# One token of gated attention and a Mish layer: the result as 256 columns in four rows, stored in 16 rows of 1 KB

## The chip, the cores and the metric

The kernel runs on one core of a Trainium2 chip. The metric is the device time of one execution in microseconds (us). The core has five engines that run side by side and wait for each other by semaphores: TensorE (PE; its weight loads are shown as PEld), VectorE (DVE), ScalarE (ACT), GpSimd (POOL) and SyncE (SP), which here only issues transfers. A transfer is split over 16 DMA engines. SBUF is the working memory of 128 partitions; TensorE writes its sums to PSUM, from where VectorE or ScalarE has to copy them before they can be stored.

## What is computed

Two branches start from the same `x` (2 batches, 512 features, float32) and are mixed by a gate:

```python
g = _sigmoid((x * gate_w).sum(-1, keepdims=True))
a = _A_ref(x, A_k_cache, A_v_cache, A_wq, A_wo)
b = _B_ref(x, B_w1, B_b1, B_w2)
return g * a + (1 - g) * b
```

`_A_ref` is attention with one query per batch: `q = x @ wq` gives 32 heads of 128, which share 8 key-value heads in fours; scores against the last 4096 positions of the key cache, softmax, the weighted sum of the values, and the product with `wo` (4096 x 512). `_B_ref` is `mish(x @ w1 + b1) @ w2` with 1792 hidden features, so `w2` is 1792 x 512. The result is 2 x 512. Some 91 MB of float32 weights and caches have to be read for it.

## The kernel before

**Loads.** SyncE issues nearly every load, in order, into three SBUF buffers of 64 KB per partition that are used in turn (`stream`): the query weights, eight pairs of keys and values, then `w12` (most of `w1`, the first part of `wo`, the first seven 128-row blocks of `w2`) and the rest of `wo`. The last loads are four pieces of `in_w2` (lines 337 to 341): rows 7 to 10 (a row here is one of the 14 blocks of 128 hidden features, 512 columns wide), rows 11 and 12, and row 13 in two halves of 128 KB each. `flat` (line 311) yields for each piece its columns and its place in the flat input. A piece with several rows has one contiguous run in memory per partition.

**Groups of columns.** All matmuls of this kernel that matter have a stationary operand of 32 columns, so that four of them go to four column groups of TensorE: group j writes partitions 32j to 32j+31 of the PSUM tile. Only two of the 32 columns hold the two batches; the others are zero (`padded`, line 108 on).

**The end.** `project` (line 349) adds up in `acc` the attention output times `wo` and the first seven rows of `w2`: here the four groups split the sum's terms, not its columns, and so `acc` holds four partial sums of 512 columns. ScalarE copies it to `asum` (line 377). A matmul with `fold2` then adds the four up. From there the groups split the result's columns: group j has columns 128j to 128j+127.

- `finish(lhsT, rhs)` (line 358) adds one row into `fin`, 128 partitions x 128 columns, with four matmuls. It is called for rows 7 to 10, for `asum`, and for row 11.
- VectorE copies `fin` to `base` (line 400).
- `half(f, h, x0, step)` (line 386) adds rows 12 and 13 into two other sums, `own_pt` and `own_q`, of 64 columns per group each. Row 13's first half is loaded ahead of its second, so that `own_pt` can be done before the last piece has come.
- `result(h)` (line 393) adds `base` and one of the two sums into `res`, on VectorE.
- The stationary operand has its two columns at the end of the 32 for even groups and at the start for odd ones (`y = j % 2 * (Q - B)`). The result thus lies in partitions 30 and 31, 32 and 33, 94 and 95, 96 and 97.
- The store (line 412) writes `res[24:104]`, 80 rows of 512 bytes; the host picks the eight rows that count. It is issued by SyncE, with a semaphore of its own, on which GpSimd waits at the very end (line 484). The `landed` instruction (line 407) lets SyncE see the last nine loads land ahead of the store.

The order of the matmuls is the order of the program where they are wrapped in `pin`. The pool `work` (line 65) has the tag `p` with two buffers, used in turn by `qs` (two), `p` (eight), `hs`, `asum` and `base`.

Of the kernel before, what the change touches and what calls it, by code (L numbers as in the profile page):

```python
# [8 lines left out]
F32 = mybir.dt.float32  # L9
AF = mybir.ActivationFunctionType  # L10
ALU = mybir.AluOpType
AX = mybir.AxisListType

P = 128
B = 2
D = 512
# [8 lines left out]
NJ = 4  # L25
NT = 4
Q = 32
# [4 lines left out]
FC = F // P  # L32
# [14 lines left out]
SCALE = DH ** -0.5  # L47
CAP = 20.0
CUTS = (0, 7, 11, 13, 14)
PART = P // 2  # L50
WO = (1, 6, 8)
ROWS = (24, 104)
WIDE = 2 * Q - B
AHEAD = W1 + WO[0] * REP * D

# [2 lines left out]
def decode_kernel(ctx: ExitStack, tc: tile.TileContext, res, stored, small, wqh, wqt, kv_in, w12, wo, w2, *rest):  # L58
    *parts, before, behind, out = rest
    nc = tc.nc  # L60
# [1 line left out]
    stream = ctx.enter_context(tc.tile_pool(name="stream", bufs=3))  # L62
    const = ctx.enter_context(tc.tile_pool(name="const", bufs=1))
    single = ctx.enter_context(tc.tile_pool(name="single", bufs=1))
    work = ctx.enter_context(tc.tile_pool(name="work", bufs=2))
    ps_s = ctx.enter_context(tc.tile_pool(name="ps_s", bufs=2, space=bass.MemoryType.PSUM))
    ps_1 = ctx.enter_context(tc.tile_pool(name="ps_1", bufs=1, space=bass.MemoryType.PSUM))

# [2 lines left out]
    def load(name, *parts):  # L71
        t = stream.tile([P, 2 * CHUNK], F32, tag="s", name=name)
        x = 0
        for cols, src in parts:
            loads.append(nc.sync.dma_start(t[:, x : x + cols], src))  # L75
            x += cols
        return t
# [36 lines left out]
    oT, actT, act2, fold2 = (padded[:, sum(sizes[:k]) : sum(sizes[: k + 1])] for k in range(len(sizes)))  # L114
    oT = oT.rearrange("p (k q) -> p k q", q=Q)
    actT = actT.rearrange("p (f q) -> p f q", q=Q)
    act2 = act2.rearrange("p (f q) -> p f q", q=WIDE)
# [41 lines left out]
    pin = tc.keep_in_program_order  # L159

    def scores(kv, t):
        sc = ps_s.tile([P, 512], F32, tag="sc", name=f"sc{kv}")
        for m in range(BN):
            for j in range(NJ):
                nc.tensor.matmul(sc[Q * j : Q * j + Q, :], qz[:, kv, m * Q : m * Q + Q],  # L165
                                 t[:, (m * NJ + j) * 512 : (m * NJ + j + 1) * 512],
                                 start=(m == 0), stop=(m == BN - 1))
        nc.vector.tensor_reduce(mx[:, kv : kv + 1], sc, axis=AX.X, op=ALU.max, negate=True)  # L168
        p = work.tile([P, 512], F32, tag="p", name=f"p{kv}")
        nc.scalar.activation(p, sc, AF.Exp, bias=mx[:, kv : kv + 1], accum_out=ls[:, kv : kv + 1])  # L170
        return p
# [125 lines left out]
    for kv in range(HKV):  # L297
        t = load(f"kv{kv}", (2 * CHUNK, kv_in[kv][:, : 2 * CHUNK]))
        p = scores(kv, t[:, :CHUNK])
# [9 lines left out]
    w12_t = load("w12", (AHEAD + CUTS[1] * D, w12))  # L309

    def flat(src, cuts, size):
        for f0, f1 in zip(cuts, cuts[1:]):
            yield (f1 - f0) * size, src[f0 * size * P : f1 * size * P].rearrange("(p x) -> p x", p=P)

    wo_t = stream.tile([P, 2 * CHUNK], F32, tag="s", name="wo")
    x = (WO[-1] - WO[0]) * REP * D
# [16 lines left out]
    x = 0  # L333
# [1 line left out]
        loads.append(nc.sync.dma_start(wo_t[:, x : x + cols], src))  # L335
        x += cols
    x = AHEAD + CUTS[1] * D
    pieces = [2 * (f - CUTS[1]) for f in CUTS[1:]]
    for cols, src in flat(w2, [*pieces[:-1], pieces[-1] - 1, pieces[-1]], D // 2):
        loads.append(nc.sync.dma_start(w12_t[:, x : x + cols], src))  # L340
        x += cols
    hidden(w12_t)
    outputs(kf, r)

    acc = ps_1.tile([P, D], F32, tag="acc", name="acc")
    fin = ps_1.tile([P, P], F32, tag="fin", name="fin")
    n_col = [0] * NJ

    def project(j, lhsT, rhs, n):
# [2 lines left out]
                                start=(n_col[j] == 1), stop=(n_col[j] == n))  # L352

    n_of = [HKV + len(range(j, CUTS[1], NJ)) for j in range(NJ)]
    n_fin = FC - CUTS[1] - 1
    done = [0]

    def finish(lhsT, rhs):
        for j in range(NJ):
            y = j % 2 * (Q - B)  # L360
            nc.tensor.matmul(fin[Q * j : Q * j + Q, :], lhsT[:, y : y + Q], rhs[:, j * P : (j + 1) * P],  # L361
                             start=(done[0] == 0), stop=(done[0] == n_fin - 1))
        done[0] += 1

    def middle(f0, f1):
        for f in range(f0, f1):
            x = AHEAD + f * D
            pin(project(f % NJ, actT[:, f, :], w12_t[:, x : x + D], n_of[f % NJ]))

    first = WO[0] * REP  # L370
# [5 lines left out]
    asum = work.tile([P, D], F32, tag="p", name="asum")  # L376
    nc.scalar.copy(asum, acc)

    def output(f0, f1):
        for f in range(f0, f1):  # L380
            x = AHEAD + f * D
            finish(act2[:, f - CUTS[1], :], w12_t[:, x : x + D])

    own = [ps_1.tile([P, PART], F32, tag=tag, name=f"own_{tag}") for tag in ("pt", "q")]

    def half(f, h, x0, step):
        for j in range(NJ):
            x, y = x0 + j * step, j % 2 * (Q - B)
            pin(nc.tensor.matmul(own[h][Q * j : Q * j + Q, :], act2[:, f - CUTS[1], y : y + Q],
                                 w12_t[:, x : x + PART], start=(f == FC - 2), stop=(f == FC - 1)))  # L390

    def result(h):
        cols = slice(h * PART, (h + 1) * PART)
        return pin(nc.vector.tensor_tensor(res[:, cols], base[:, cols], own[h], op=ALU.add))

    output(CUTS[1], CUTS[2])
    finish(fold2, asum)
    output(CUTS[2], FC - 2)
    base = work.tile([P, D], F32, tag="p", name="base")[:, :P]
    pin(nc.vector.tensor_copy(base, fin))  # L400
    for h in range(2):
        half(FC - 2, h, AHEAD + (FC - 2) * D + h * PART, P)
    for h in range(2):
        half(FC - 1, h, AHEAD + (FC - 1) * D + h * D // 2, PART)
        copy = result(h)

    landed = nc.sync.nop()
    for ld in loads[-9:]:
        tc.add_manual_dep(landed.ins, ld.ins.name,
                          mybir.DependencyInfo(mybir.DependencyClass.Sync, mybir.DependencyReason.DATA),  # L410
                          reason="SyncE sees the last loads land ahead of the store")
    store = nc.sync.dma_start(out, res[ROWS[0] : ROWS[1]]).then_inc(stored, 16)
    tc.no_tile_sem_insts.add(store.ins.name)
# [76 lines left out]
```

## Time and profile before

| | us |
|---|---|
| time, median of 3 runs (lowest to highest) | 218.78 (218.69 to 218.85) |
| the profiled execution | 218.85 |
| its span, first to last instruction | 217.0 |
| PE busy | 117.1 (54%) |
| DVE busy | 22.0 (10%) |
| ACT busy | 15.5 (7%) |
| POOL busy | 11.4 (5%) |
| moved by DMA | 91.38 MB, mean 421 GB/s |

Times in the profile are from the start of the span. A busy engine is not necessarily one that matters: the chain of waits tells which work ended last, and idle time of an engine off that chain costs nothing. In a row of the timeline stand the start, the time from there to the end of the group, the engine, the line of the program, the operation, what it writes and reads, the shape, and in brackets the idle time before it and what ended it. A group merges like instructions that follow each other, and groups can overlap. In a row of the windows stand, behind the window's length, the busy time of PE, PEld, DVE, ACT and POOL with their counts, the granted TensorE clock as a share of full speed, the share of the DMA engines that was busy, and GB/s.

### The profile page before, as it was taken

The page shows a single profiled execution, that of the slowest core. Times are in us where ns is not written, and L with a number is a line of the kernel's source. Part 1 is how long each engine was busy: PE and PEld are TensorE (multiplying, and loading weights), DVE is VectorE, ACT ScalarE, POOL GpSimd, SP SyncE. Part 2 cuts the span into 40 slices and gives each one's busy share as a digit, 9 for nine tenths or more (in the row PEclk, how much of TensorE's full clock was granted, in tenths as well). Part 3 has the DMA queues.
Part 4 walks back from the last instruction along what each step waited for, and adds up shares of the span by engine and source line. Part 5 has one row for each costly group of instructions (what it writes and reads, how often), then busy time and mean ns, then how long its engine had stood idle before and what let it go on. Part 6 is the DMA issues. An engine that isn't in the chain of part 4 may idle for free.

```text
span 217.0 us, 1884 instructions
## 1 busy us (share of the span) xinstructions
PE 117.1 (54%) x836; PEld 34.2 (16%) x836; DVE 22.0 (10%) x35; ACT 15.5 (7%) x34; POOL 11.4 (5%) x34
## 2 busy tenths in 40 slices
PE   0000786277046609543863754186166819769995
PEld 0000221012011102100120110012011201224333
DVE  0000000010001230100105010010501000260101
ACT  0200011011001000200020020002001000301001
POOL 8000100000000000000000000000000050101200
PEclk9999999589959985995669699669757697999699
DMA  9798988899989998999999899989998999999894
GB/s 362 338 507 351 571 387 387 387 559 399 399 387 544 411 399 387 532 414 399 399 519 414 387 423 459 471 387 423 450 471 387 435 447 437 422 385 468 381 404 162
DMA packets 2896, 91.38 MB, mean 421 GB/s; under 512 B 582, under 2 KB 918, under 8 KB 1098
## 3 DMA queue, kind: packets, MB, share of 16 engines
q1 hardware_dynamic: 2746, 91.24, 97.7%
q8 instruction: 6, 0.10, 0.2%
q0 software_dynamic: 144, 0.05, 0.1%
HBM read 91.24 MB, written 0.04 MB: 421 GB/s over the span
## 4 chain that ended last, share of the span: by engine, by line
DMA 76%; PE 17%; ACT 2%; SPq 2%; DVE 1%; issue 1%; POOL 1%; DVEq 0%; ACTq 0%
DMA kv<-in_kv 60%; DMA w<-in_w 16%; PE sc L165 8%; PE o L189 6%; ACT p L170 1%; DVE mx L168 1%; SPq L322 1%; PE pp L177 1%; ACT pT L178 1%; PE fin L361 1%; POOL wo L318 1%; SPq L335 0%; SPq L75 0%; SPq L81 0%; DVE base L400 0%
## 5 line engine op out<-in xcount | busy, mean ns | idle before, releaser
L165 PE MATMUL sc<-kv,qz 128*32 128x512 f32 x256 | 46.0, 884 | 51.5 <-DMA kv<-in_kv 51.5
L189 PE MATMUL o<-kv,pT 128*32 128x512 f32 x256 | 32.5, 647 | 5.8 <-ACT pT L178 5.8
L165 PEld LDWEIGHTS sc<-kv,qz 128*32 128x32 f32 x256 | 10.2, 155 | 86.2 <-DMA kv<-in_kv 58.1
L145 PE MATMUL qp<-wq,x 128*32 128x512 f32 x64 | 10.7, 712 | 23.0 <-POOL x L108 23.0
L168 DVE TENSOR_REDUCE mx<-sc 128x1 f32<-128x512 f32 x8 | 5.5, 691 | 113.2 <-PE sc L165 113.2
L170 ACT ACTIVATE p<-sc,mx 128x512 f32<-128x512 f32 x8 | 5.5, 687 | 133.5 <-DVE mx L168 133.5
L177 PE MATMUL pp<-ident,p 128*128 128x128 f32 x32 | 5.2, 286 | 12.1 <-ACT p L170 12.1
L189 PEld LDWEIGHTS o<-kv,pT 128*32 128x32 f32 x256 | 7.7, 117 | 23.5 <-issue 15.7
L318 POOL MEMSET wo<- 128x1536 f32 x1 | 1.4, 1377 | 147.6 <-PE o L189 147.6
L199 DVE TENSOR_REDUCE od<-om 128x256 f32<-128x1024 f32 x4 | 7.6, 1906 | 0.1
L196 DVE TENSOR_TENSOR om<-o,pick 128x1024 f32<-128x1024 f32 x4 | 4.9, 1225 | 20.7 <-PE o L189 20.7
L351 PE MATMUL acc<-wo,padded 128*32 128x512 f32 x56 | 6.8, 597 | 0.0
L145 PEld LDWEIGHTS qp<-wq,x 128*32 128x32 f32 x64 | 2.3, 127 | 28.1 <-POOL x L108 23.0
L177 PEld LDWEIGHTS pp<-ident,p 128*128 128x128 f32 x32 | 3.3, 140 | 19.0 <-ACT p L170 19.0
L178 ACT COPY pT<-pp 128x512 f32<-128x512 f32 x8 | 4.7, 585 | 6.2 <-PE pp L177 6.2
L351 PE MATMUL acc<-w,padded 128*32 128x512 f32 x22 | 4.5, 904 | 0.4 <-DVE padded L243 0.4
L260 PE MATMUL hp<-w,x 128*32 128x512 f32 (+1 forms) x30 | 3.6, 540 | 1.8 <-DMA w<-in_w 1.8
L351 PEld LDWEIGHTS acc<-wo,padded 128*32 128x32 f32 x56 | 2.3, 112 | 4.4 <-issue 2.8
L260 PE MATMUL hp<-wo,x 128*32 128x512 f32 x6 | 2.7, 592 | 0.0
L151 PE MATMUL qt<-ident,qs 128*128 128x128 f32 x8 | 1.3, 286 | 1.4 <-ACT qs L148 1.4
L127 DVE TENSOR_REDUCE xs<-xg 128x2 f32<-128x8 f32 x1 | 0.2, 161 | 18.2 <-POOL xg L125 18.2
L241 PE MATMUL ol<-kf,od 128*128 128x8 f32 x16 | 1.9, 253 | 0.0
(78 smaller groups left out, 35.0 us busy)
## 6 DMA issues: line engine op xcount, KB each, us to landing
wq<-in_wqt SPq DMA_DIRECT2D x1, 7168.0 KB, 21.3
w<-in_w SPq DMA_DIRECT2D x1, 6144.0 KB, 40.6
wo<-in_wo SPq DMA_DIRECT2D x1, 5120.0 KB, 27.9
wo<-in_wo SPq DMA_DIRECT2D x1, 2048.0 KB, 32.3
wq<-in_wqh SPq DMA_DIRECT2D x1, 1024.0 KB, 4.9
w<-in_w SPq DMA_DIRECT2D x1, 1024.0 KB, 34.3
w<-in_w SPq DMA_DIRECT2D x1, 512.0 KB, 35.0
w<-in_w SPq DMA_DIRECT2D x2, 128.0 KB, 21.2
```

The lines of the kernel that those rows point to most:

```text
L145: nc.tensor.matmul(qp[Q * k : Q * k + Q, :], x32[:, c, :], w[:, c, k, :], start=(c == 0), stop=(c == DC - 1))
L165: nc.tensor.matmul(sc[Q * j : Q * j + Q, :], qz[:, kv, m * Q : m * Q + Q], t[:, (m * NJ + j) * 512 : (m * NJ + j + 1) * 512], start=(m == ...
L168: nc.vector.tensor_reduce(mx[:, kv : kv + 1], sc, axis=AX.X, op=ALU.max, negate=True)
L170: nc.scalar.activation(p, sc, AF.Exp, bias=mx[:, kv : kv + 1], accum_out=ls[:, kv : kv + 1])
L177: pin(nc.tensor.transpose(pp[:, c, :], p[:, c * P : (c + 1) * P], ident))
L178: nc.scalar.copy(pT, pp)
L189: pin(nc.tensor.matmul(o[Q * j : Q * j + Q], pT[:, c, Q * j : Q * j + Q], t[:, (c * NJ + j) * 512 : (c * NJ + j + 1) * 512], start=(c == 0 ...
L196: nc.vector.tensor_tensor(ov, pair[0].rearrange("p k (m d) -> p k m d", m=BN), pick[:, None, :, None].to_broadcast([P, 2, BN, DH]), op=ALU ...
L199: nc.vector.tensor_reduce(od[:, kv - 1 : kv + 1], ov.rearrange("p k m d -> p k d m"), axis=AX.X, op=ALU.add)
L260: nc.tensor.matmul(hp[Q * j : Q * j + Q, :n], x32[:, c, :], w[:, :n], start=(c == 0), stop=(c == (DC + SLOTS if j in away else DC) - 1))
L318: nc.gpsimd.memset(ext, 0.0)
L351: return nc.tensor.matmul(acc[Q * j : Q * j + Q, :], lhsT, rhs, start=(n_col[j] == 1), stop=(n_col[j] == n))
```

## The change

The result is split over two column groups of 256 columns (`NO`, `DO`), not four of 128. Its columns lie in two PSUM sums for the whole tail, `fins`: 192 columns per group in one and 64 in the other (`PARTS`). Every row from 7 to 13, and `asum`, is added into both sums, with two matmuls each. There is no `base` any more, and no addition: when the sums are complete, VectorE copies the 192 columns into `res` and ScalarE the 64. Row 13 is loaded as 192 KB (for the first sum) and 64 KB (for the second). The result lies in partitions 30 to 33; the store writes `res[24:40]`, 16 rows of 1 KB. `res` is 256 columns wide, and the `work` pool has one buffer instead of two. All matmuls of the tail are now wrapped in `pin`.

```diff
-PART = P // 2
+NO = 2
+DO = D // NO
+PARTS = ((0, 192), (192, 64))
 WO = (1, 6, 8)
-ROWS = (24, 104)
+ROWS = (24, 40)
...
-    work = ctx.enter_context(tc.tile_pool(name="work", bufs=2))
+    work = ctx.enter_context(tc.tile_pool(name="work", bufs=1))
...
-    pieces = [2 * (f - CUTS[1]) for f in CUTS[1:]]
-    for cols, src in flat(w2, [*pieces[:-1], pieces[-1] - 1, pieces[-1]], D // 2):
+    pieces = [(f - CUTS[1]) * D for f in CUTS[1:]]
+    for cols, src in flat(w2, [*pieces[:-1], pieces[-1] - NO * PARTS[1][1], pieces[-1]], 1):
...
-    def finish(lhsT, rhs):
-        for j in range(NJ):
-            y = j % 2 * (Q - B)
-            nc.tensor.matmul(fin[Q * j : Q * j + Q, :], lhsT[:, y : y + Q], rhs[:, j * P : (j + 1) * P],
-                             start=(done[0] == 0), stop=(done[0] == n_fin - 1))
-        done[0] += 1
...
-    own = [ps_1.tile([P, PART], F32, tag=tag, name=f"own_{tag}") for tag in ("pt", "q")]
-
-    def half(f, h, x0, step):
-        for j in range(NJ):
+    fins = [ps_1.tile([P, n], F32, tag=tag, name=f"fin_{tag}") for tag, (_, n) in zip(("fin", "pt"), PARTS)]
+
+    def finish(lhsT, src, h, x0, step, first=False, last=False):
+        for j in range(NO):
             x, y = x0 + j * step, j % 2 * (Q - B)
-            pin(nc.tensor.matmul(own[h][Q * j : Q * j + Q, :], act2[:, f - CUTS[1], y : y + Q],
-                                 w12_t[:, x : x + PART], start=(f == FC - 2), stop=(f == FC - 1)))
-
-    def result(h):
-        cols = slice(h * PART, (h + 1) * PART)
-        return pin(nc.vector.tensor_tensor(res[:, cols], base[:, cols], own[h], op=ALU.add))
-
-    output(CUTS[1], CUTS[2])
-    finish(fold2, asum)
-    output(CUTS[2], FC - 2)
-    base = work.tile([P, D], F32, tag="p", name="base")[:, :P]
-    pin(nc.vector.tensor_copy(base, fin))
-    for h in range(2):
-        half(FC - 2, h, AHEAD + (FC - 2) * D + h * PART, P)
-    for h in range(2):
-        half(FC - 1, h, AHEAD + (FC - 1) * D + h * D // 2, PART)
-        copy = result(h)
+            pin(nc.tensor.matmul(fins[h][Q * j : Q * j + Q, :], lhsT[:, y : y + Q],
+                                 src[:, x : x + PARTS[h][1]], start=first, stop=last))
+
+    for f in range(CUTS[1], FC - 1):
+        if f == CUTS[2]:
+            for h, (c, _) in enumerate(PARTS):
+                finish(fold2, asum, h, c, DO)
+        for h, (c, _) in enumerate(PARTS):
+            finish(act2[:, f - CUTS[1], :], w12_t, h, AHEAD + f * D + c, DO, first=f == CUTS[1])
+    for h, (c, n) in enumerate(PARTS):
+        finish(act2[:, FC - 1 - CUTS[1], :], w12_t, h, AHEAD + (FC - 1) * D + NO * c, n, last=True)
+    pin(nc.vector.tensor_copy(res[: NO * Q, : PARTS[0][1]], fins[0][: NO * Q]))
+    copy = pin(nc.scalar.copy(res[: NO * Q, PARTS[0][1] :], fins[1][: NO * Q]))
...
-    args.append(nc.dram_tensor("out_0", (ROWS[1] - ROWS[0], P), F32, kind="ExternalOutput").ap())
+    args.append(nc.dram_tensor("out_0", (ROWS[1] - ROWS[0], DO), F32, kind="ExternalOutput").ap())
```

`output` and the accumulator `fin` of 128 columns go with the lines taken away. On the host, row 13 of `w2` is laid out as the first 192 columns of both halves of 256, then the last 64 of both.

More of the change, by code (lines that the diff above doesn't have):

```diff
@@ L345, in decode_kernel @@
     acc = ps_1.tile([P, D], F32, tag="acc", name="acc")
-    fin = ps_1.tile([P, P], F32, tag="fin", name="fin")
     n_col = [0] * NJ
@@ L354, in decode_kernel @@
     n_of = [HKV + len(range(j, CUTS[1], NJ)) for j in range(NJ)]
-    n_fin = FC - CUTS[1] - 1
-    done = [0]
-    def finish(lhsT, rhs):
-        for j in range(NJ):
-            y = j % 2 * (Q - B)
-            nc.tensor.matmul(fin[Q * j : Q * j + Q, :], lhsT[:, y : y + Q], rhs[:, j * P : (j + 1) * P],
-                             start=(done[0] == 0), stop=(done[0] == n_fin - 1))
-        done[0] += 1
     def middle(f0, f1):
@@ L377, in decode_kernel @@
     nc.scalar.copy(asum, acc)
[L379 to L382, printed above, removed]
-    own = [ps_1.tile([P, PART], F32, tag=tag, name=f"own_{tag}") for tag in ("pt", "q")]
-    def half(f, h, x0, step):
-        for j in range(NJ):
-            x, y = x0 + j * step, j % 2 * (Q - B)
-            pin(nc.tensor.matmul(own[h][Q * j : Q * j + Q, :], act2[:, f - CUTS[1], y : y + Q],
-                                 w12_t[:, x : x + PART], start=(f == FC - 2), stop=(f == FC - 1)))
-    def result(h):
-        cols = slice(h * PART, (h + 1) * PART)
-        return pin(nc.vector.tensor_tensor(res[:, cols], base[:, cols], own[h], op=ALU.add))
-    output(CUTS[1], CUTS[2])
-    finish(fold2, asum)
-    output(CUTS[2], FC - 2)
-    base = work.tile([P, D], F32, tag="p", name="base")[:, :P]
-    pin(nc.vector.tensor_copy(base, fin))
-    for h in range(2):
-        half(FC - 2, h, AHEAD + (FC - 2) * D + h * PART, P)
-    for h in range(2):
-        half(FC - 1, h, AHEAD + (FC - 1) * D + h * D // 2, PART)
-        copy = result(h)
+    fins = [ps_1.tile([P, n], F32, tag=tag, name=f"fin_{tag}") for tag, (_, n) in zip(("fin", "pt"), PARTS)]
+    def finish(lhsT, src, h, x0, step, first=False, last=False):
+        for j in range(NO):
+            x, y = x0 + j * step, j % 2 * (Q - B)
+            pin(nc.tensor.matmul(fins[h][Q * j : Q * j + Q, :], lhsT[:, y : y + Q],
[10 more added lines that the diff above has]
+    copy = pin(nc.scalar.copy(res[: NO * Q, PARTS[0][1] :], fins[1][: NO * Q]))
     landed = nc.sync.nop()
@@ L455 @@
     w2_0 = w2[: CUTS[1]].transpose(1, 0, 2).reshape(P, CUTS[1] * D)
-    last = w2[FC - 1].reshape(P, NJ, 2, PART).transpose(2, 0, 1, 3).ravel()
-    w2 = np.concatenate([*(w2[f:t].transpose(1, 0, 2).ravel() for f, t in zip(CUTS[1:], CUTS[2:-1])), last])
+    last = w2[FC - 1].reshape(P, NO, DO)
+    w2 = np.concatenate([*(w2[f:t].transpose(1, 0, 2).ravel() for f, t in zip(CUTS[1:], CUTS[2:-1])),
+                         *(last[:, :, x : x + n].ravel() for x, n in PARTS)])
     wo = a("A_wo").reshape(HQ, DH, D)
@@ L477 @@
             for n, t in arrays.items()]
-    args.append(nc.dram_tensor("out_0", (ROWS[1] - ROWS[0], P), F32, kind="ExternalOutput").ap())
+    args.append(nc.dram_tensor("out_0", (ROWS[1] - ROWS[0], DO), F32, kind="ExternalOutput").ap())
     stored = nc.alloc_semaphore("stored")
     start = -(-nc.sbuf_base // 32) * 8
-    res = nc.alloc_sbuf_tensor("res", [P, P + (-start - P) % 256], F32).ap()[:, :P]
+    res = nc.alloc_sbuf_tensor("res", [P, DO + (-start - DO) % 256], F32).ap()[:, :DO]
     with tile.TileContext(nc) as tc:
@@ L486 @@
     r = run_bass_kernel_spmd(nc, [{f"in_{n}": t for n, t in arrays.items()}], core_ids=[0])
-    rows = [Q * j + (1 - j % 2) * (Q - B) - ROWS[0] for j in range(NJ)]
+    rows = [Q * j + (1 - j % 2) * (Q - B) - ROWS[0] for j in range(NO)]
     o = np.stack([r.results[0]["out_0"][x : x + B] for x in rows])
```

## The prediction

> **What bounds the kernel now.** I read the page's DMA row first, then the chain, then the last 5 us of the timeline, since every edit but one lies there.
>
> ```profile
> DMA  9798988899989998999999899989998999999894
> ...
> DMA kv<-in_kv 60%; DMA w<-in_w 16%; PE sc L165 8%; PE o L189 6%; ACT p L170 1%; DVE mx L168 1%; SPq L322 1%; PE pp L177 1%; ACT pT L178 1%; PE fin L361 1%; POOL wo L318 1%; SPq L335 0%; SPq L75 0%; SPq L81 0%; DVE base L400 0%
> ```
>
> Each digit is a fortieth of the span: the 16 DMA engines are busy in nearly all of it until the last 5 us. The chain is mostly waits for loads. So the kernel ends when the stream has ended, plus what must still be done after it. The next rows are that end: the piece of the chain that comes just before it, TensorE's and VectorE's rows of the timeline, and SyncE's: the store, `landed`'s wait for the last loads (line 407), and its part in the program's closing barrier.
>
> ```profile
> 178.51 34.32 DMA w<-in_w
> ```
>
> ```profile
> 212.97 1.08 PE L361 MATMUL fin<-w,padded 128*32 128x128 f32 x32 [0.61 <-DMA w<-in_w]
> 213.84 0.43 PE L361 MATMUL fin<-asum,padded 128*32 128x128 f32 x8
> 214.10 0.43 PE L361 MATMUL fin<-w,padded 128*32 128x128 f32 x8
> 214.34 0.29 PE L389 MATMUL own_pt<-w,padded 128*32 128x64 f32 x8
> 214.45 0.29 PE L389 MATMUL own_q<-w,padded 128*32 128x64 f32 x8
> 214.56 0.29 PE L389 MATMUL own_pt<-w,padded 128*32 128x64 f32 x8
> 214.77 0.32 PE L389 MATMUL own_q<-w,padded 128*32 128x64 f32 x8
> ```
>
> ```profile
> 214.66 0.29 DVE L400 COPY base<-fin 128x128 f32<-128x128 f32 x1 [12.63 <-PE fin L361]
> 215.06 0.22 DVE L394 TENSOR_TENSOR res<-base,own_pt 128x64 f32<-128x64 f32 x1
> 215.19 0.21 DVE L394 TENSOR_TENSOR res<-base,own_q 128x64 f32<-128x64 f32 x1
> ```
>
> ```profile
> 215.43 0.35 SPq L412 DMA_DIRECT2D out<-res  x1
> L407 SPq EVENT_SEMAPHORE  x4: 28/28/20535, 194.2 to 214.9; - x4
> L482 SPq EVENT_SEMAPHORE  x5: 17/17/28, 215.8 to 216.8; - x5
> ```
>
> TensorE waits 0.61 us for the first piece of `in_w2` (rows 7 to 10), which lands at 178.51 + 34.32 = 212.83. From there it works as the pieces come in. The wait of L407 began at 194.2 and took 20.5 us, so the last piece landed near 214.7, and the last `own_q` group starts at 214.77. TensorE is thus just abreast of the stream: what stands behind the last landing is one group of 64 columns, one addition, the store, and the wait for it until 217.0. Between the first piece and that last group lie 214.77 - 212.97 = 1.80 us. That is all the room TensorE has in this tail before it, and not the stream, sets the end.
>
> **TensorE's new tail.** In the rows, x8 is four matmuls, since a float32 matmul shows as two passes. The four matmuls of a row of `w2` go to four column groups (partitions 32j on), and these run beside each other. From 212.97 to 213.84 four rows of 128 columns pass: 8 passes per group, 0.109 us each. At 64 columns it is two passes from 214.34 to 214.45: 0.055 us each. So time goes by columns per group, 0.85 ns each. Whether fewer groups run faster is told by the place where one group runs alone, the end of the hidden layer:
>
> ```profile
> 196.66 1.88 PE L260 MATMUL hp<-wo,x 128*32 128x512 f32 x4
> 197.09 0.11 PEld L260 LDWEIGHTS hp<-wo,x 128*32 128x32 f32 x1 [0.32 <-issue]
> 197.52 0.11 PEld L260 LDWEIGHTS hp<-wo,x 128*32 128x32 f32 x1 [0.32 <-issue]
> ...
> 207.82 0.20 PEld L351 LDWEIGHTS acc<-wo,padded 128*32 128x32 f32 x4 [0.23 <-issue]
> 208.25 0.20 PEld L351 LDWEIGHTS acc<-wo,padded 128*32 128x32 f32 x4 [0.23 <-issue]
> ```
>
> Alone, a pass of 512 columns comes every 0.43 us (197.09 to 197.52); with four groups at work a pass of all four comes every 0.43 us too (207.82 to 208.25). A group neither gains nor loses by its neighbours. The change uses two groups of 256 columns instead of four of 128. The number of instructions per row stays at 8, but each group now streams twice the columns: two passes of 192 (0.109 + 0.055 = 0.164 us) and two of 64 (0.055), that is 2 x (0.164 + 0.055) = 0.437 us a row in place of 0.218.
>
> The tail has seven such units (rows 7 to 10, `asum`, rows 11 and 12) and then row 13. It starts at 212.97 as before: the first piece is still rows 7 to 10, 1 MB, behind the same loads. Seven units: 212.97 + 7 x 0.437 = 216.03. Row 13: two passes of 192, to 216.36, then two of 64, the last starting at 216.36 + 0.055 = 216.41. A pass of 64 takes 0.22 us from start to end (the rows of lines 361 and 389 just below, in ns), so the smaller sum is complete at 216.63, against 214.77 + 0.32 = 215.09 for `own_q`. The larger sum's last pass starts at 216.03 + 0.164 = 216.19 and takes 0.27 (128 columns) plus about 0.055: 216.52.
>
> ```profile
> L361 PE MATMUL fin<-w,padded x40: 270/273/297, 213.0 to 214.3; 128*32 128x128 f32 x40
> L389 PE MATMUL own_pt<-w,padded x16: 219/219/219, 214.3 to 214.6; 128*32 128x64 f32 x16
> 198.58 0.37 ACT L264 COPY hs<-hp 128x256 f32<-128x256 f32 x1 [11.33 <-PE hp L260]
> 212.42 0.58 ACT L377 COPY asum<-acc 128x512 f32<-128x512 f32 x1 [11.81 <-PE acc L351]
> ```
>
> **The copies.** The first addition and the copy to `base` lay beside TensorE's work; only the second addition was on the path. In its place stand two copies side by side. VectorE's is 192 wide, which no row shows: 64 took 0.21 us and 128 took 0.29, so 192 about 0.36 (bounds 0.29 and 0.45). It starts 0.10 us after the sum (215.09 to 215.19), at 216.62, and ends at 216.98. ScalarE's is 64 wide: 256 took 0.37 us and 512 took 0.58, so 64 about 0.21 (bounds 0.15 and 0.37). It starts by 216.73 and ends at 216.94. Both engines idle there. The store named only ScalarE's copy as what it waits for; should it wait for VectorE's too, 0.04 us are added. I take 216.96 for 215.41: **+1.55 us**.
>
> **The store.** It has 16 rows of 1 KB, not 80 of 512 bytes, 40 KB down to 16.
>
> ```profile
> out<-res SPq DMA_DIRECT2D x1, 40.0 KB, 1.5
> 215.43:216.28 0.85, 0.00 (x0) 0.00 (x0) 0.00 (x0) 0.00 (x0) 0.00 (x0) 1.00 0.00 0
> 216.28:216.60 0.32, 0.00 (x0) 0.00 (x0) 0.00 (x0) 0.00 (x0) 0.00 (x0) 1.00 0.51 128
> 216.60:217.00 0.40, 0.00 (x0) 0.00 (x0) 0.00 (x0) 0.00 (x0) 0.00 (x0) 1.00 0.00 0
> ```
>
> Of the 1.5 us the data move in 0.32; 0.85 before and 0.40 after are start and confirmation. One packet per engine instead of five can take at most some 0.25 of the 0.32. Beyond 0.2 it would buy nothing anyway: the program's closing barrier (L482) goes on until 216.8, and it starts from the same SyncE. Bounds 0 and -0.25; I take **-0.15 us**. [...]
>
> **What costs nothing.** The last row comes as 192 KB and 64 KB, not twice 128 KB: as many issues on SyncE's queue and as many bytes, landing near 214.7, while row 13 isn't begun before 216.03. So 1.3 us cover it, and would still cover a last piece that came later by packets of half the size. The `landed` waits end at 214.9, well ahead of the store. Nothing moves past a queue: POOL and SyncE issue what they did. The `work` pool has one buffer, not two, so each write of `qs`, `p`, `hs` and `asum` must wait for the transposes of the one before.
>
> ```profile
> 31.22 0.66 PE L151 MATMUL qt<-ident,qs 128*128 128x128 f32 x4 [0.71 <-ACT qs L148]
> 35.52 0.60 ACT L148 ACTIVATE qs<-qp 128x512 f32<-128x512 f32 x1 [4.35 <-PE qp L145]
> ...
> 185.55 0.66 PE L177 MATMUL pp<-ident,p 128*128 128x128 f32 x4 [0.54 <-ACT p L170]
> ```
>
> The tightest are these two: the first transposes are done at 31.9, 3.6 us before the second `qs`; those of the last `p` at 186.2, 12 us before `hs` (198.58). Those between repeat once per 8 MB load. That buffers lie elsewhere in memory may change the stream's pace; no row shows it, and 1 KB of `res` is little against tiles of 64 KB per partition. I take 0, with 0.2 us either way.
>
> **Sum.** 1.55 - 0.15 = +1.40. The profiled execution took 218.85 (a span of 217.0 and 1.85 around it), so it would be 220.25; the median, 218.78, lies 0.07 lower: **220.2 us**.
>
> **Rivals.** *TensorE keeps up.* If two groups shared what four shared, each would stream at double pace, a row would stay at 0.218 us and the stream would set the end. It decides at 1.80 / 7 = 0.257 us a unit: below it TensorE is done before the last landing. Then the last piece is four instructions at 214.77, done at 215.07 or so; ScalarE's copy ends at 215.38, the store saves its 0.15, and the time is 218.85 - 0.03 - 0.15, about 218.6, faster or the same. For it: 8 instructions a row as before. Against it: the lone group, at 0.43 us for 512 columns. 5%.
>
> *Order costs more.* If a matmul had to start behind all earlier ones, the second group's first pass would go beside the first group's second pass and the small matmul wait behind it: 0.164 x 3 + 0.055 = 0.55 us a unit, nearly 0.11 more over eight, 221.1. Against it: the same order would have taken 16 x 0.109 = 1.74 us for the four rows that took 0.87 to the next group's start. The Trainium skill (TensorE: Matmul & The Clock Gate, Part 3) has matmuls start and end strictly in program order; by these rows passes of different groups do not queue like that. 3%.
>
> *The clock.* TensorE's granted clock was 1.00 throughout the tail:
>
> ```profile
> 212.97:214.05 1.08, 1.08 (x40) 1.02 (x40) 0.00 (x0) 0.03 (x1) 0.00 (x0) 1.00 0.70 257
> 180.28 0.21 PEld L165 LDWEIGHTS sc<-kv,qz 128*32 128x32 f32 x4 [0.64 <-issue]
> 181.13 0.21 PEld L165 LDWEIGHTS sc<-kv,qz 128*32 128x32 f32 x4 [0.64 <-issue]
> ```
>
> Elsewhere passes come every 0.85 us (180.28 to 181.13), at half pace. If that fell on the tail, 3.4 us would be added: 223.7. The wait ahead of it is only 0.61 us. 3%.
>
> **How the numbers follow.** The forecast 86%, the rivals 5, 3 and 3, and 3% for a moved stream. The low end is 220.2 less 0.1 (store), 0.15 (copies), 0.2 (stream) and 0.15 for the first piece landing earlier: 219.6. The high end adds 0.15, 0.1 and 0.2 likewise: 220.7. A measurement of this kernel tells about 0.2%, or 0.44 us, from no change; the whole range is above that. Slower 0.92, same 0.04, faster 0.04.
>
> **What would show it.** `fin` from 212.97 to about 216.4 with no wait for a load behind the first; passes of 192 columns 0.164 us apart; SyncE's `landed` done 1.5 us or more before the store; the store's issue near 217.0 and its landing 0.1 to 0.2 us sooner after it. I am wrong if rows go at less than 0.26 us, or if TensorE waits again for the last piece.

## The result, and the profile after

| | before | changed |
|---|---|---|
| time, median of 6 runs (lowest to highest), us | 218.83 (218.69 to 218.96) | 220.36 (220.28 to 220.51) |
| the profiled execution, us | 218.85 | 220.51 |
| its span, us | 217.0 | 218.4 |

The changed kernel is slower: 1.0072 times the time before, with a 95% interval from 1.0062 to 1.0082, or 1.53 us in the medians. The forecast was 220.2 with a range from 219.6 to 220.7.

The timeline of the changed kernel, TensorE's rows of the tail (the rows between are the same again, unit by unit):

```profile
212.88 0.52 PE L375 MATMUL fin_fin<-w,padded 128*32 128x192 f32 x4 [0.62 <-DMA w<-in_w]
213.20 0.31 PE L375 MATMUL fin_pt<-w,padded 128*32 128x64 f32 x4
213.31 0.52 PE L375 MATMUL fin_fin<-w,padded 128*32 128x192 f32 x4
...
214.62 0.52 PE L375 MATMUL fin_fin<-asum,padded 128*32 128x192 f32 x4
...
215.93 0.52 PE L375 MATMUL fin_fin<-w,padded 128*32 128x192 f32 x4
216.25 0.31 PE L375 MATMUL fin_pt<-w,padded 128*32 128x64 f32 x4
```

There is one wait, for the first piece, and none after it. From 212.88 to row 13 at 215.93 seven units take 3.05 us, 0.436 each; the forecast had 0.437. The last group of matmuls starts at 216.25 (its second passes 0.055 us later), where that of the kernel before started at 214.77.

The rest of the tail from the same timeline, then SyncE's wait for the last loads (line 389, which was 407), and the end of the program (line 467, which was 484):

```profile
216.49 0.35 DVE L386 COPY res<-fin_fin 64x192 f32<-64x192 f32 x1 [14.55 <-PE fin_fin L375]
216.60 0.20 ACT L387 COPY res<-fin_pt 64x64 f32<-64x64 f32 x1 [3.64 <-PE fin_pt L375]
216.93 0.35 SPq L394 DMA_DIRECT2D out<-res  x1
```

```profile
L389 SPq EVENT_SEMAPHORE  x4: 17/28/20527, 194.1 to 214.8; - x4
L467 POOLq EVENT_SEMAPHORE  x1: 17/17/17, 218.4 to 218.4; - x1
```

The last loads were seen at 214.8, as before. The store went out at 216.93, 2.1 us later; it had followed the last landing by about 0.7 us. So the stream isn't what ends last any more: TensorE is.

The store itself, in three windows (columns as in the prediction: busy time of five engines, clock, DMA share, GB/s):

```profile
216.93:217.78 0.85, 0.00 (x0) 0.00 (x0) 0.00 (x0) 0.00 (x0) 0.00 (x0) 1.00 0.00 0
217.78:218.02 0.24, 0.00 (x0) 0.00 (x0) 0.00 (x0) 0.00 (x0) 0.00 (x0) 1.00 0.28 69
218.02:218.41 0.39, 0.00 (x0) 0.00 (x0) 0.00 (x0) 0.00 (x0) 0.00 (x0) 1.00 0.00 0
```

The start and the confirmation are what they were, 0.85 and 0.39; the transfer took 0.24 us in place of 0.32. Added up between the two profiled executions: first piece 0.09 sooner (212.88 for 212.97), from there to the end of the copies 3.96 for 2.44 (+1.52), from there to the store's issue 0.09 for 0.03 (+0.07), the store 1.48 for 1.55 (-0.07). That is +1.43, the difference of the spans.

### The profile page after: what moved, and what is told of

It reads as the page before. It is cut to its first block, busy times and chain, and to the rows that moved or that the text cites. A ratio compares the mean times of both kernels' runs of the same rounds, so it can differ in the third digit from the quotient of the medians.

```text
span 218.4 us, 1858 instructions
## 1 busy us (share of the span) xinstructions
PE 118.3 (54%) x820; PEld 35.0 (16%) x820; DVE 21.7 (10%) x33; ACT 15.7 (7%) x35; POOL 11.4 (5%) x34
## 4 chain that ended last, share of the span: by engine, by line
DMA 77%; PE 16%; SPq 2%; ACT 2%; DVE 1%; issue 1%; POOL 1%; ACTq 0%
DMA kv<-in_kv 61%; DMA w<-in_w 17%; PE sc L167 8%; PE o L191 5%; PE fin_fin L375 1%; ACT p L172 1%; SPq L324 1%; DVE mx L170 1%; PE pp L179 1%; ACT pT L180 1%; POOL wo L320 1%; SPq L77 0%; SPq L337 0%; PE fin_pt L375 0%; SPq L83 0%
## 5 line engine op out<-in xcount | busy, mean ns | idle before, releaser
L375 PE MATMUL fin_fin<-w,padded 128*32 128x192 f32 x28 | 3.2, 327 | 0.6 <-DMA w<-in_w 0.6
L375 PE MATMUL fin_pt<-w,padded 128*32 128x64 f32 x28 | 2.2, 219 | 0.0
```

What stands on the lines that cost most here:

```text
L375: pin(nc.tensor.matmul(fins[h][Q * j : Q * j + Q, :], lhsT[:, y : y + Q], src[:, x : x + PARTS[h][1]], start=first, stop=last))
```

## The experiments

The theory: two column groups stream twice the columns each, and TensorE's own time from the first piece on is the end. The rivals: the two copies and their waits; the number of instructions, or that only two groups work; the single buffer of `work`; the store. Each kernel was timed beside the kernel before on the same chip (218.73 to 218.78 there).

### Four groups again, the rest of the change kept

```diff
-NO = 2
+NO = 4
-PARTS = ((0, 192), (192, 64))
+PARTS = ((0, 96), (96, 32))
-ROWS = (24, 40)
+ROWS = (24, 104)
```

> The changed kernel with four column groups of 128 columns again (sums of 96 and 32 columns per group, the store 80 rows of 512 bytes), but still without base and additions. Theory (TensorE's tail doubled because each of two groups streams twice the columns; that alone is the loss): a unit takes 0.22 us again, TensorE is abreast of the loads, the last group of matmuls starts at about 214.8 behind the last landing, and the time is 218.8, within 0.15 us of the kernel before. Rival (the two copies and their two waits, or the moved buffers, make the loss): 220.0 to 220.4.

Measured: 219.29 us, 1.0018 times the kernel before (1.0009 to 1.0027). Two thirds of the loss are gone, but not all, and neither theory nor rival had named 219.29. The profile tells the two apart. Its timeline, and the store's row among the DMA issues:

```profile
213.05 0.37 PE L375 MATMUL fin_fin<-w,padded 128*32 128x96 f32 x8 [0.83 <-DMA w<-in_w]
...
215.43 0.35 SPq L394 DMA_DIRECT2D out<-res  x1
...
out<-res SPq DMA_DIRECT2D x1, 40.0 KB, 1.9
```

The store is issued at 215.43, exactly when it was in the kernel before, though the first piece came 0.08 us later. So up to the issue the theory holds: with four groups nothing is lost, and the two copies and waits cost no more than the addition did. But the same store of 40 KB took 1.9 us to land instead of 1.5. In the trace 15 of its 16 confirmations arrive by 216.90 and one at 217.37. Just before, at a time when no load was left, one of the 16 DMA engines was busy:

```profile
214.80:215.20 0.40, 0.29 (x23) 0.16 (x9) 0.12 (x1) 0.03 (x1) 0.00 (x0) 1.00 0.00 0
215.20:216.28 1.08, 0.00 (x0) 0.00 (x0) 0.14 (x1) 0.16 (x1) 0.00 (x0) 1.00 0.06 15
...
q8 instruction: 7, 0.11, 0.2%
```

A share of 0.06 is one engine of 16, and 15 GB/s over 1.08 us are 16 KB. The queue named instruction has seven packets, one more than the six of the kernel before, and the trace's record of it runs from 215.37 to 216.33. This became the next question (below, more code).

### Half of the columns in two groups

```diff
+    turns = [0, 0]
+
     def finish(lhsT, src, h, x0, step, first=False, last=False):
+        n = PARTS[h][1] // 2
+        z = turns[h] % 2 * n
+        turns[h] += 1
         for j in range(NO):
-            x, y = x0 + j * step, j % 2 * (Q - B)
-            pin(nc.tensor.matmul(fins[h][Q * j : Q * j + Q, :], lhsT[:, y : y + Q],
-                                 src[:, x : x + PARTS[h][1]], start=first, stop=last))
+            x, y = x0 + j * step + z, j % 2 * (Q - B)
+            pin(nc.tensor.matmul(fins[h][Q * j : Q * j + Q, z : z + n], lhsT[:, y : y + Q],
+                                 src[:, x : x + n], start=first, stop=last))
```

> The changed kernel, each matmul of the tail over only half of its columns (96 and 32 instead of 192 and 64, the two halves of a sum in turn), so half of the terms of the result are left out; groups, number of instructions, copies, loads and the store stay. Theory: a unit falls from 0.437 to 0.22 us, TensorE waits for the last pieces again, the sums are complete at about 215.0, and the time is 218.7 (218.5 to 218.9). Rival (instructions, or that only two groups work, set the pace): the time stays within 0.15 us of 220.36.

Measured: 219.01 us, 1.0023 (1.0007 to 1.0039); the profiled execution took 218.72. Its timeline:

```profile
212.84 0.36 PE L380 MATMUL fin_fin<-w,padded 128*32 128x96 f32 x4 [0.59 <-DMA w<-in_w]
...
214.00 0.36 PE L380 MATMUL fin_fin<-w,padded 128*32 128x96 f32 x4
...
214.49 0.36 PE L380 MATMUL fin_fin<-w,padded 128*32 128x96 f32 x4
214.68 0.25 PE L380 MATMUL fin_pt<-w,padded 128*32 128x32 f32 x4
...
215.34 0.35 SPq L399 DMA_DIRECT2D out<-res  x1
```

The same groups, instructions, copies and store, half the columns, and TensorE is abreast of the loads again: the store leaves 1.59 us sooner than in the changed kernel. That rules out the instructions and the two groups as such, and the copies. The median lies 0.1 above the expected bounds; a part of that is the single buffer (below). Three of its twelve runs took 220.1 to 220.2 us at a mean granted clock of 0.82, where 0.85 is usual. None of these three was profiled; an execution with such a clock is seen in the run with one sum.

### The first piece in two

```diff
-CUTS = (0, 7, 11, 13, 14)
+CUTS = (0, 7, 9, 11, 13, 14)
...
-        if f == CUTS[2]:
+        if f == CUTS[3]:
...
-    for ld in loads[-9:]:
+    for ld in loads[-10:]:
```

> The changed kernel with the first piece of the last weights cut into rows 7 and 8 and rows 9 and 10, one load more. Theory (from the first piece's landing on, the end is TensorE's own time): TensorE can begin at about 212.4, right behind the projection, not at 212.88, and has rows 9 and 10 in time; all that follows shifts by 0.45 us and the time is 219.9 (219.8 to 220.05). Rival (the end is set by the last landing or by what follows it): no change, 220.36, or a little more for the added load.

Measured: 219.65 us, 1.0034 (1.0021 to 1.0047), so 0.89 us over the kernel before where the changed kernel had 1.53. From its timeline:

```profile
212.37 0.50 PE L375 MATMUL fin_fin<-w,padded 128*32 128x192 f32 x4
...
216.41 0.35 SPq L394 DMA_DIRECT2D out<-res  x1
```

And SyncE's wait for the last loads:

```profile
L389 SPq EVENT_SEMAPHORE  x4: 17/28/28, 215.0 to 215.1; - x4
```

TensorE has no wait at all here and begins 0.51 us sooner; the store goes out 0.52 us sooner, although the last loads were seen at 215.1, which is 0.3 us later than in the changed kernel. The end hangs on TensorE's start, one to one, while the last landing has no say. The gain in time, 0.64 us with each kernel held against the kernel before, was larger than the 0.45 expected: TensorE could start 0.06 earlier than assumed, and a tenth is not explained.

### The kernel before, with a store of 16 rows

```diff
-ROWS = (24, 104)
+ROWS = (24, 40)
...
-    rows = [Q * j + (1 - j % 2) * (Q - B) - ROWS[0] for j in range(NJ)]
+    rows = [Q * j + (1 - j % 2) * (Q - B) - ROWS[0] for j in (0, 1, 0, 1)]
```

> The kernel before with a store of 16 rows of 512 bytes, not 80; columns 256 to 511 of the result are left out. Theory (the store's fixed parts are nearly all of it; the changed kernel's profile has 1.44 us from issue to landing where 1.51 stood): 0.05 to 0.1 us less than the kernel before, which shows in the profile more than in the time. Rival (descriptors count, 0.25 us): 218.6 or less. A second rival: the closing barrier ends last anyway and the span gains nothing.

Measured: 218.66 us, 0.9993 (0.9985 to 1.0002). Its timeline, and the store's row among the DMA issues:

```profile
215.33 0.35 SPq L412 DMA_DIRECT2D out<-res  x1
...
out<-res SPq DMA_DIRECT2D x1, 8.0 KB, 1.4
```

From the store's issue (215.33) to the end of the span (216.75) it is 1.41 us, 0.14 less than in the kernel before; in the time 0.1 at most. The span still ends 0.04 us behind the last confirmation, as in the kernel before, so the closing barrier isn't what ends last. A smaller store saves something, but little. Packets and bytes both fell to a fifth, so this run doesn't tell their costs apart; 16 rows of 512 bytes were confirmed 0.06 us sooner than the changed kernel's 16 rows of 1 KB.

### The kernel before, with one buffer

```diff
-    work = ctx.enter_context(tc.tile_pool(name="work", bufs=2))
+    work = ctx.enter_context(tc.tile_pool(name="work", bufs=1))
```

> The kernel before with one buffer in the work pool instead of two, nothing else. Theory (every writer of that buffer comes 3 us or more behind the transposes of the one before, and the shifted buffers leave the loads' pace alone): within 0.1 us of the kernel before. Rival (the single buffer or the shift costs): 0.2 us or more slower.

Measured: 218.92 us, 1.0009 (1.0000 to 1.0018), 0.19 over the kernel before. That lies between theory and rival, and the span tells more than the time: its median is 216.9, the same as beside it. What grew is the time outside the span, 2.08 us in the median for 1.87. Every kernel here with one buffer has 1.98 to 2.09 outside, and every one with two has 1.87 to 1.89. So nobody waits for the buffer, as predicted, and the loads keep their pace, but the edit isn't free. What runs there isn't shown. In the profiled executions of six of the seven kernels with one buffer, the trace has an 8 KB load of instructions that starts 1.8 to 1.9 us behind the last instruction. No kernel with two buffers has it. With it the profiled executions had 1.90 to 2.10 us outside their spans, without it 1.86 to 1.91, so it may be a part of that time, and no more can be said. The edit also lengthens ScalarE's program: with one buffer the trace has eight semaphore instructions more there (59 or 60 instructions on ScalarE in all seven kernels, 51 or 52 in the four others). That these bring the load fits, but no run tests it, and why the time outside grows stays open.

### Both copies on VectorE

```diff
-    copy = pin(nc.scalar.copy(res[: NO * Q, PARTS[0][1] :], fins[1][: NO * Q]))
+    copy = pin(nc.vector.tensor_copy(res[: NO * Q, PARTS[0][1] :], fins[1][: NO * Q]))
```

> The changed kernel with both copies on VectorE, one behind the other. Theory: the 64-wide copy follows the 192-wide one, which ended at 216.84, and ends at about 217.05; SyncE waits for one engine rather than two and is 0.06 us quicker, so the store goes out 0.1 to 0.15 us later and the time is 220.45 to 220.55. Rival (the second engine saves nothing, its wait costs as much as it hides): 220.36 or less.

Measured: 220.41 us, 1.0080 (1.0068 to 1.0093). It can't be told from the changed kernel's 1.0072. Its timeline:

```profile
216.34 0.35 DVE L386 COPY res<-fin_fin 64x192 f32<-64x192 f32 x1 [14.40 <-PE fin_fin L375]
216.62 0.20 DVE L387 COPY res<-fin_pt 64x64 f32<-64x64 f32 x1
216.85 0.35 SPq L394 DMA_DIRECT2D out<-res  x1
```

The store's issue follows the start of the first copy by 0.51 us, where it was 0.44: the second copy begins 0.28 us behind the first, before that one's 0.35 are over, and SyncE, which waits for one engine only, issues the store 0.03 us behind the last copy instead of 0.09. The second engine saves 0.07 us, less than the 0.1 to 0.15 that the theory had.

### More code: the kernel before with 96 TensorE instructions more

```diff
-        for c in range(NT):
+        for c in (*range(NT),) * (4 if 1 <= kv <= 4 else 1):
             pin(nc.tensor.transpose(pp[:, c, :], p[:, c * P : (c + 1) * P], ident))
```

> The kernel before with 48 transposes more, repeated in four key-value steps in the middle where TensorE waits for loads: 96 TensorE instructions of 64 bytes (as many as the four groups with two sums have more than the kernel before), none of them near the end. Theory (code comes in blocks of 16 KB, 256 instructions, and the end of TensorE's program has moved over the start of a block): an instruction load appears between 213 and 216, the store's last confirmation comes 0.3 to 0.5 us later (issue to landing 1.8 to 2.0 us), and the time is 219.1 to 219.3. Rival (that load and the late store of the four groups have nothing to do with each other, or the load doesn't move): 218.7 to 218.85, and issue to landing 1.5.

Measured: 219.17 us, 1.0024 (1.0015 to 1.0032). The steps with the repeated transposes are done 85 us and more before the end. Yet the end is later. Its timeline, the store's row among the DMA issues, and the windows around the tail:

```profile
214.62 0.32 PE L389 MATMUL own_q<-w,padded 128*32 128x64 f32 x8
...
215.30 0.35 SPq L412 DMA_DIRECT2D out<-res  x1
...
out<-res SPq DMA_DIRECT2D x1, 40.0 KB, 1.7
```

```profile
214.60:214.80 0.20, 0.20 (x18) 0.16 (x8) 0.20 (x1) 0.00 (x0) 0.00 (x0) 1.00 0.00 0
214.80:216.10 1.30, 0.14 (x8) 0.00 (x0) 0.37 (x3) 0.00 (x0) 0.00 (x0) 1.00 0.05 13
```

The store is issued 0.13 us sooner than in the kernel before, and takes 1.7 us instead of 1.5. In front of it stands a load of 16 KB (13 GB/s over 1.30 us), which the trace's record puts from 214.92 to 216.00. In the kernel before, the last such load starts at 209.8, and TensorE has 200 instructions left; here and with the four groups it starts where TensorE has 3 left. So the theory on the instruction load holds: TensorE's code comes in blocks of 16 KB, and a block that starts near the end puts its load into one DMA engine just ahead of the store's packets. As with the four groups, one of the store's 16 confirmations is late: 15 arrive by 216.80 and one at 217.05. How the load delays it isn't shown, for the load's record ends at 216.00 and the store's packets run from 216.16 to 216.46. The median time rose as expected, by 0.39 us. The landing, 1.7 us, fell short of the expected 1.8 to 2.0: the profiled execution, the shortest of the eleven, shows 0.24 in the store, and the rest wasn't seen.

### Four groups, one sum, one copy

```diff
-    fins = [ps_1.tile([P, n], F32, tag=tag, name=f"fin_{tag}") for tag, (_, n) in zip(("fin", "pt"), PARTS)]
+    fin = ps_1.tile([P, DO], F32, tag="fin", name="fin")
...
+            finish(act2[:, f - CUTS[1], :], w12_t, 0, DO, AHEAD + f * D, DO, first=f == CUTS[1])
+    for c, n in PARTS:
+        finish(act2[:, FC - 1 - CUTS[1], :], w12_t, c, n, AHEAD + (FC - 1) * D + NO * c, n, last=c > 0)
+    copy = pin(nc.vector.tensor_copy(res, fin))
```

With `NO`, `PARTS` and `ROWS` as for the first experiment; `finish` takes columns c to c + n of the one sum.

> The changed kernel with four column groups of 128 columns, all in one PSUM sum and one copy by VectorE behind the last matmul; the store has 80 rows of 512 bytes; row 13 in parts of 96 and 32 columns. It has 36 matmuls in the tail (64 in the four groups with two sums, 40 in the kernel before, 32 in the changed one). Theory (the four groups keep abreast of the loads; what the four groups with two sums lost was a 16 KB load of instructions that ran from 215.37 to 216.33 on one DMA engine, in front of the store): no such load after 210, issue to landing of the store 1.5 us, the copy ends at about 215.4 and the time is 218.75 to 218.9. Rival (the other layout of buffers or the tail's form costs the 0.5 us): 219.2 to 219.4.

Measured: 218.89 us, 1.0005 (0.9996 to 1.0014), not to be told from the kernel before. With 36 matmuls in the tail the last instruction load starts at 211.07, in a tail that ran later than usual (below), and the store takes 1.5 us:

```profile
q8 instruction: 6, 0.10, 0.2%
...
out<-res SPq DMA_DIRECT2D x1, 40.0 KB, 1.5
```

This is the changed kernel's plan without its two column groups, and the loss is gone. It doesn't beat the kernel before either. Whether the additions it saves were worth anything can't be told, since it also carries the single buffer, which alone cost 0.19 us.

Its profiled execution was one of its longer ones, 219.95 us, and shows a different end. Windows of that execution, then of the kernel before:

```profile
205.00:208.00 3.00, 3.00 (x16) 0.58 (x11) 0.00 (x0) 0.00 (x0) 0.00 (x0) 0.50 1.01 431
```

```profile
205.00:208.00 3.00, 3.00 (x27) 1.17 (x25) 0.00 (x0) 0.00 (x0) 0.00 (x0) 0.84 1.01 431
```

The clock was at 0.50 in the projection, 16 passes fit where 27 had, and the projection's sum was copied at 214.42 instead of 212.42. TensorE then no longer kept up. So the place where the clock is low, which differs by execution, reaches the end of these kernels too.

### The kernel before, with two stores

```diff
-    store = nc.sync.dma_start(out, res[ROWS[0] : ROWS[1]]).then_inc(stored, 16)
...
+    for engine, (r0, o0) in ((nc.sync, (24, 0)), (nc.scalar, (88, 16))):
+        store = engine.dma_start(out[o0 : o0 + 16], res[r0 : r0 + 16]).then_inc(stored, 16)
```

> The kernel before with two stores of 16 rows of 512 bytes, one issued by SyncE and one by ScalarE, that leave out the 48 rows between. Theory (a store of 16 rows confirms 0.14 us sooner than one of 80; two side by side cost little more): 0.05 to 0.13 us faster, 218.62 to 218.7. Rival (the second issue or its place in the closing barrier takes it back): 218.75 or more.

Measured: 218.81 us, 1.0002 (0.9989 to 1.0015): no gain. The two are issued side by side, and the last of 32 confirmations comes 1.55 us after the first issue, where the one store of 80 rows had 1.51:

```profile
215.35 0.35 SPq L413 DMA_DIRECT2D out<-res  x1
215.36 0.41 ACTq L413 DMA_DIRECT2D out<-res  x1
```

The second issue takes back what the fewer rows gave; the rival was right.

## Why the prediction was right

**TensorE's tail.** This was the sum's main term, and it came out as worked out: 0.436 us a unit for 0.437, the last pass 3.43 us behind the first for 3.44. The lone column group of the hidden layer was the right row to read: a group's pace depends on its own columns, not on its neighbours. Half the columns brought the end back with everything else kept, and the four groups brought the store's issue back to 215.43.

**The room.** The 1.80 us between the first piece and the last group decided it. With 0.257 us a unit as the limit and 0.436 needed, TensorE became what ends last, and the start of TensorE moved the end one to one (first piece in two). The rival that TensorE keeps up fell with it, and so did the one by strict order: the two groups' passes stood side by side in the profile, without the 0.11 us a unit. The clock's rival did not come up: the store's windows and the tail's passes show full pace.

**The copies.** 0.35 and 0.20 us for the estimates of 0.36 and 0.21. They began 0.04 us after their sums, not 0.10, but the wait for a second engine took 0.07 us (0.09 from the last copy to the issue; 0.03 with both copies on VectorE), where the prediction had added 0.04 at most for it. Together: copies and issue 0.04 us later than assumed against the first piece's start, hidden by the first piece's coming 0.09 sooner. The store's issue was forecast for about 216.98 and came at 216.93.

**The store.** Mis-sized: -0.15 was taken, and -0.07 measured. The bounds, 0 and -0.25, held it, and 0 would have been as near as the value taken. The transfer of 0.32 us was shortened by only 0.08; the 0.85 us ahead of the first packet and the 0.39 behind the last stayed. The Trainium skill (DMA: Bandwidth & Descriptors, "Anatomy of one DMA — SWDGE (gpsimd) path") puts most of the fixed time of a DMA that GpSimd issues into the write's confirmation. This store, issued by SyncE, has more of it ahead of the first packet, and no run here stores by GpSimd.

**What was said to cost nothing.** The last piece's other cut and the `landed` waits did. The single buffer did not: it costs about 0.15 to 0.2 us outside the span, which the prediction had only as an allowance of 0.2 for the loads' pace, and that pace wasn't the reason. The span grew by 1.43, close to the sum's 1.40, and the medians by 1.53; the 0.10 between lies outside the span. That the span came so near is in part luck: the first piece 0.09 sooner, the copies and the issue 0.04 later and the store's missing 0.08 cancel to 0.03.

**What the sum left out.** Nothing in it asked where TensorE's code ends. The changed kernel has 32 matmuls in its tail for 40, so it stayed clear of the block's start that the first experiment met; that was luck.

## What to carry to other kernels

When a tail runs abreast of the last loads, count the room TensorE has there and compare it with columns per column group, not with instructions: giving up two of four column groups doubled the time of this stream of small matmuls, from 0.218 to 0.436 us a row, and a store cheaper by 0.07 us doesn't pay for it. Read the pace of a lone group from a row of the same profile where only one is at work. When a variant with more instructions is slower than its timeline explains, look at the instruction queue before blaming the edit.

## What was not expected of the hardware

- A 16 KB load of instructions, about 1 us on one DMA engine, just ahead of a store delays the store's last confirmation by 0.24 to 0.43 us (more code, four groups). Adding 48 transposes 85 us and more before the end was enough to bring it there.
- Pool buffers can change the time outside the span: one buffer instead of two raised it from 1.87 to 2.08 us, with the span unchanged. The cause is open.
- Two copies on one engine overlapped: the second began 0.28 us after the first, which lasted 0.35. The two additions of the kernel before had done the same (215.06 for 0.22 us, then 215.19).
